# Loading the first K tiles of w_in by 64-partition DMAs, with new instruction orders, in a fused attention and MoE kernel

## The chip, the cores and the metric

The kernel runs on one core of a Trainium2 chip. The metric is the device time of one execution in microseconds (us), lower is better. A run counts as slow when it is over 1.5% above the fastest of the same kernel in its call. Engines are called as the profile calls them: PE (TensorE matmul), PEld (its weight loads), DVE (VectorE), ACT (ScalarE), POOL (GpSimd), SP (SyncE). DMA engines, sixteen of them, are separate from these; a load issued by POOL is carried by some or all of the sixteen.

## The reference, cut to what matters

```python
def _attn_ref(q, k, v, g_q, g_k):                 # 8 batches, 12 heads, 448 rows, 64 columns
    q_n, k_n = rmsnorm(q, g_q), rmsnorm(k, g_k)
    scores = q_n @ k_n.T / 8
    ...                                           # softmax over the last axis
    return attn @ v

def _moe_ref(x, w_in, w_out, alpha):              # x: (8 * 448, 768) from the attention's output
    h = x @ w_in                                  # w_in: (768, 2048)
    g = h + sin(alpha * h) ** 2 / (alpha + 1e-9)
    return g @ w_out                              # w_out: (2048, 768)
```

## The kernel before

The kernel works batch by batch. In each of eight stages PE does the scores and the attention of one batch, and between them ("fillers") the second product `g @ w_out` of the batch before. At the end of the stage stands the first product `x @ w_in` of this batch, 96 matmuls of 128 x 448. Weights are loaded once, in stage 0, beside the attention of batch 0. The f32 weights are cast to bf16 on the way, and POOL issues these loads.

```python
    def load_w_in(half, c):          # half of the 2048 columns; c: which pair of the six K tiles
        cols = slice(half * D_FF // 2, (half + 1) * D_FF // 2)
        rows = moe_w_in[c * 2 * P:(c + 1) * 2 * P, cols]
        if c:
            nc.gpsimd.dma_start(out=w_in_sb[half][:, 2 * c:2 * c + 2], in_=rows.rearrange("(p x) f -> p x f", x=2))
        else:
            for pp in range(2):
                nc.gpsimd.dma_start(out=w_in_sb[half][:, pp], in_=rows.rearrange("(hi pp d) f -> pp hi d f", hi=2, pp=2)[pp])
```

For K tiles 0 and 1 the rows of `w_in` must stand in the order in which the attention leaves its heads: partition `hi * 64 + d` of K tile `pp`. Seen from DRAM one such K tile is two blocks of 64 rows, 128 rows apart.

```python
    def first_product(b, beside):
        ORDER = (0, 1, 2, 4, 3, 5)   # K tiles 0 and 1 of four column blocks first, then 2, 4, 3, 5
        ...                          # then column blocks 4 to 15, all K tiles of each
```

The order of instructions on every engine is written out by hand, as a string of tokens for stage 0, stage 1 and the later stages. The tokens that matter here:

```python
# S: scores of one tile and their exp.  A number or f: so many filler steps (8 matmuls each).
# W00: load_w_in(0, 0); W10: load_w_in(1, 0).   q50, q51: POOL squares q, k of chunk 5.
# u50, u51: DVE sums these squares.   k30, k31: POOL multiplies by the inverse root (2 instructions "qkn" each).
STAGE_N = (
    ...
        "r3 q41 f f 1 l5 1 f S 3 u40 1 S S 5 S S u41 o7 v7 S S 5 S 2 q51 k31 f S 2 S q50 k30 2 S g4 1 u50 "
        "S 2 r4 t3 1 S z3 x7 k40 y7 z1 z2 z1 "
    ...
```

When the last filler step of a block is done, DVE evicts its PSUM banks into `osb` with a copy and an add; the banks are then free for PE's next use. DVE runs its instructions in the order of the program.

Of the kernel before, what the change touches and what calls it, by code (L numbers as in the profile page):

```python
# [17 lines left out]
try:  # L18
# [13 lines left out]
STAGE_0 = (  # L32
    (
        "L G b11 q00 u00 q01 g0 b15 r00 u01 k00 r01 D1 k01 V00 q11 u11 p00 q10 V02 W11 p011 S4 u10 q20 r1 "
        "g1 S4 q21 S1 l3 u20 S1 k11 k10 S4 u21 S g2 r2 p1 k20 S2 V01 S2 S o3 q30 W00 S W12 k21 l4 o4 D2 "
        "q40 W01 p2 l5 S1 g4 S u30 q31 W02 g3 u40 v1 q41 S v6 u31 S W10 S S3 S1 S3 x2 S S x1 S1 u41 x2 y2 "
        "q51 y3 x2 z1 z1 y2 z1 z1 q50 r4 r3 z2 z1 O00 k31 "
    ),
    "2122130230213212301301321032130132012120312031230",
# [1 line left out]
)  # L41
STAGE_1 = (
    (
        "q30 6 r2 1 S 4 S S 3 S 2 u30 S k21 1 q41 1 S 1 f S 1 k20 1 S 1 S 1 f 1 S 1 f f f S q31 p2 1 u31 "
        "f l5 S 2 g3 S 2 S r3 2 u41 k30 V10 S 1 q40 1 V11 q50 S o7 v7 1 S k31 1 u40 S 3 S 2 S S 1 x6 r4 "
        "k41 z2 q51 x1 t3 y7 z5 "
    ),
    "13230103120101013131312310202302301230123",
    {-1: 'g4 V12', 1: 'k40', 3: 'u50 g5', 5: 'l6 u51', 8: 't4 l7'},
)  # L50
STAGE_N = (
    (
        "1 r2 q31 q30 f 2 S V10 f 3 V11 f f 2 S k20 3 S 2 k21 S u31 q40 1 t2 2 S 1 f u30 g3 S 2 f S f S "
        "r3 q41 f f 1 l5 1 f S 3 u40 1 S S 5 S S u41 o7 v7 S S 5 S 2 q51 k31 f S 2 S q50 k30 2 S g4 1 u50 "
        "S 2 r4 t3 1 S z3 x7 k40 y7 z1 z2 z1 "
    ),
    "01232302102020301301320321310130210231023",
    {-1: 'l6 u51 V12', 1: 'k41', 2: 't4 l7', 3: 'g5'},
# [10 lines left out]
def kernel(  # L69
# [23 lines left out]
    nc = tc.nc  # L93
    B, H, S, D = q.shape
# [104 lines left out]
    w_in_sb = [wpool.tile([P, KT, D_FF // 2], BF16, name=f"w_in_{half}") for half in range(2)]  # L199
# [21 lines left out]
    def load_w_in(half, c):  # L221


        cols = slice(half * D_FF // 2, (half + 1) * D_FF // 2)
        rows = moe_w_in[c * 2 * P:(c + 1) * 2 * P, cols]
        if c:
            nc.gpsimd.dma_start(out=w_in_sb[half][:, 2 * c:2 * c + 2], in_=rows.rearrange("(p x) f -> p x f", x=2))
        else:
            for pp in range(2):
                nc.gpsimd.dma_start(out=w_in_sb[half][:, pp], in_=rows.rearrange("(hi pp d) f -> pp hi d f", hi=2, pp=2)[pp])  # L230

    def load_w_out(half, part):
        src = moe_w_out.rearrange("(mt p) d -> p mt d", p=P)
# [275 lines left out]
    def step(b, token):  # L509
# [6 lines left out]
        elif what == "L":  # L516
            spread_alpha()
        elif what == "W":
            load_w_in(*n)
        elif what == "O":  # L520
            load_w_out(*n)
# [85 lines left out]
```

## Time and profile before

| what | value |
|---|---|
| time, median | 430.05 us (428.12 to 430.5) |
| span of the profiled execution | 429.9 us |
| PE busy | 408.5 us, 95% |
| DVE, ACT, POOL busy | 53%, 74%, 67% |
| share of PE in the chain of waits | 84% |
| mean granted PE clock | 0.988 |

A PE that is busy 95% is the bound; the other engines matter where PE stands still. The prediction shows those places. Two more lines of before are needed, from the view of the DMA issues. Columns: what is written from what, the issuing queue, the operation and count, the KB of one load as written, and the median us from issue to landing.

```profile
w_in<-in_moe_w_in_dram POOLq DMA_DIRECT2D x4, 512.0 KB, 17.5
w_in<-in_moe_w_in_dram POOLq DMA_DIRECT2D x4, 256.0 KB, 16.5
```

The 256 KB loads are K tiles 0 and 1. They take nearly as long as loads of twice the size.

### The profile page before, as it was taken

The page shows a single profiled execution, that of the slowest core. Times are in us where ns is not written, and L with a number is a line of the kernel's source. Part 1 is how long each engine was busy: PE and PEld are TensorE (multiplying, and loading weights), DVE is VectorE, ACT ScalarE, POOL GpSimd, SP SyncE. Part 2 cuts the span into 40 slices and gives each one's busy share as a digit, 9 for nine tenths or more (in the row PEclk, how much of TensorE's full clock was granted, in tenths as well). Part 3 has the DMA queues.
Part 4 walks back from the last instruction along what each step waited for, and adds up shares of the span by engine and source line. Part 5 has one row for each costly group of instructions (what it writes and reads, how often), then busy time and mean ns, then how long its engine had stood idle before and what let it go on. Part 6 is the DMA issues. An engine that isn't in the chain of part 4 may idle for free.

```text
span 429.9 us, 14999 instructions
## 1 busy us (share of the span) xinstructions
PE 408.5 (95%) x6657; PEld 239.5 (56%) x6657; DVE 227.5 (53%) x335; ACT 316.8 (74%) x465; POOL 285.9 (67%) x269
## 2 busy tenths in 40 slices
PE   4998699999999999989999899999999999999996
PEld 2443257765576556655576356665576456665563
DVE  3775257644764466545563456645665455335511
ACT  3698188896889688976889388896889588886600
POOL 4999199799796688596794677786795785003300
PEclk9999699999999999999999899999999999999999
DMA  8899999576365643835375742837465510420022
GB/s 257 179 226 163 203 162 226 131 121 155 113 134 148 173 133 62 188 88 146 105 126 143 136 127 64 180 111 159 130 95 156 122 44 3 119 58 2 1 74 73
DMA packets 68485, 54.08 MB, mean 126 GB/s; under 512 B 39860, under 2 KB 64196, under 8 KB 68420
## 3 DMA queue, kind: packets, MB, share of 16 engines
q1 hardware_dynamic: 51378, 39.60, 35.4%
q0 software_dynamic: 16096, 11.82, 19.0%
q10 hardware_dynamic: 946, 1.70, 1.1%
q8 instruction: 52, 0.85, 0.8%
q14 instruction: 13, 0.11, 0.1%
HBM read 45.62 MB, written 11.01 MB: 132 GB/s over the span
## 4 chain that ended last, share of the span: by engine, by line
PE 84%; DMA 6%; POOL 3%; DVE 2%; ACT 2%; issue 1%; POOLq 0%; SPq 0%
PE hps L400 34%; PE ops L479 27%; PE av L360 10%; PE sc L334 6%; PE ops L460 5%; DMA w_in<-in_moe_w_in_dram 4%; POOL sq L264 2%; PE ps L242 2%; ACT expT L337 2%; DMA qk<-in_q_dram 1%; DMA small<-in_moe_alpha_dram 1%; POOL qkn L289 1%; PE tp L312 1%; DVE ms L270 1%; DVE osb L486 1%
## 5 line engine op out<-in xcount | busy, mean ns | idle before, releaser
L337 ACT ACTIVATE expT<-sc 128x896 bf16<-128x896 f32 x168 | 144.6, 918 | 15.6 <-PE sc L334 14.9
L400 PE MATMUL hps<-xT,w_in 128*128 128x448 bf16 x768 | 149.8, 357 | 6.0 <-DMA w_in<-in_moe_w_in_dram 6.0
L479 PE MATMUL ops<-w_out_sb,g_sb 64*64 64x384 bf16 x3072 | 146.1, 323 | 0.0
L386 DVE SCALAR_TENSOR_TENSOR g_sb<-s,inv_alpha_sb,hps 128x448 bf16<-128x448 f32 x128 | 81.2, 677 | 74.3 <-POOL s L381 73.8
L400 PEld LDWEIGHTS <-w_in 128*128 128x128 bf16 x768 | 75.0, 99 | 80.7 <-DMA w_in<-in_moe_w_in_dram 8.0
L378 ACT ACTIVATE s<-hps,alpha_sb 128x448 f32<-128x448 f32 x128 | 74.5, 626 | 54.1 <-PE hps L400 50.3
L381 POOL TENSOR_TENSOR s<-s 128x448 f32<-128x448 f32 x64 | 59.4, 932 | 82.3 <-ACT s L378 59.3
L479 PEld LDWEIGHTS <-g_sb 64*64 64x64 bf16 x3072 | 89.8, 107 | 39.3 <-issue 2.2
L264 POOL TENSOR_TENSOR sq<-qk 128x896 f32<-128x896 f32 x44 | 73.6, 1678 | 28.3 <-DMA qk<-in_k_dram 27.6
L289 POOL TENSOR_TENSOR qkn<-qk,inv 128x448 bf16<-128x448 f32 x80 | 73.0, 937 | 4.0 <-ACT inv L280 2.0
L334 PE MATMUL sc<-qkT 64*64 64x448 bf16 x672 | 56.9, 351 | 0.4 <-DVE qkT L319 0.2
L270 DVE TENSOR_REDUCE ms<-sq 128x14 f32<-128x896 f32 x44 | 47.0, 1079 | 16.8 <-POOL sq L264 16.8
L485 DVE COPY osb<-ops 128x384 f32<-128x384 f32 x48 | 26.7, 556 | 48.8 <-PE ops L479 48.8
L267 POOL TENSOR_TENSOR qk<-qk,gg 128x896 f32<-128x896 f32 x24 | 50.2, 2090 | 2.3 <-ACT g_sb L261 2.2
L360 PE MATMUL av<-expT,vb 64*32 64x448 bf16 (+1 forms) x1120 | 38.1, 362 | 4.3 <-DVE osb L486 4.3
L372 DVE TENSOR_TENSOR xT<-av,rec 128x896 bf16<-128x896 f32 x24 | 25.5, 1088 | 30.2 <-ACT rec L366 24.0
L383 ACT ACTIVATE s<-s 128x448 f32<-128x448 f32 x64 | 36.9, 577 | 3.0
L360 PEld LDWEIGHTS <-vb 64*32 64x32 bf16 (+1 forms) x1120 | 19.2, 97 | 19.1 <-DVE osb L486 6.4
L334 PEld LDWEIGHTS <-qkT 64*64 64x64 bf16 x672 | 20.2, 106 | 13.3 <-issue 4.5
L486 DVE TENSOR_TENSOR osb<-osb,ops 128x384 f32<-128x384 f32 x48 | 26.6, 554 | 1.7
L360 PE MATMUL av<-expT,ones 64*32 64x448 bf16 (+1 forms) x672 | 25.3, 350 | 0.2 <-ACT expT L337 0.2
L460 PE MATMUL ops<-w_out_sb,g_sb 128*128 128x384 bf16 x128 | 21.0, 326 | 0.0
(48 smaller groups left out, 186.4 us busy)
## 6 DMA issues: line engine op xcount, KB each, us to landing
out_dram<-osb SPq DMA_DIRECT2D x39, 192.0 KB, 3.4
qk<-in_q_dram SPq DMA_DIRECT2D x16, 448.0 KB, 4.5
qk<-in_k_dram SPq DMA_DIRECT2D x14, 448.0 KB, 5.2
qk<-in_q_dram SPq DMA_DIRECT2D x16, 224.0 KB, 4.6
qk<-in_k_dram SPq DMA_DIRECT2D x16, 224.0 KB, 4.9
vb<-in_v_dram POOLq DMA_DIRECT2D x16, 224.0 KB, 4.8
w_out_sb<-in_moe_w_out_dram POOLq DMA_DIRECT2D x4, 768.0 KB, 13.0
out_dram<-osb SPq DMA_DIRECT2D x26, 96.0 KB, 3.1
```

The source lines that it names most:

```text
L264: nc.gpsimd.tensor_mul(st.sq[w], qk[ci][:, w], qk[ci][:, w])
L267: eng.tensor_mul(qk[ci][:, 0], qk[ci][:, 0], gg.to_broadcast([P, 2 * NJ, D]))
L270: nc.vector.reduce_sum(st.ms[:, w, :], st.sq[w], axis=AX.X)
L289: eng.tensor_mul(n[:, :, hi, :], x[:, hi], inv[:, hi].unsqueeze(2).to_broadcast([P, NJ, D]))
L334: nc.tensor.matmul(sc[pp * 64:pp * 64 + 64, hi, :S], qkt[r, 1, j * REST:(j + 1) * REST], qkt[r, 0, :], start=True, stop=True)
L337: nc.scalar.activation(expT[c, j], sc[:, :, :S], ACT.Exp, scale=SCALE)
L360: nc.tensor.matmul(av[o, k, :S], w, expT[b * NC + c, j][r, hi, :], start=(j == 0), stop=(j == NJ - 1))
L378: nc.scalar.activation(s1, hps, ACT.Sin, scale=alpha_sb[:, m, :])
L381: nc.gpsimd.tensor_mul(s2, s1, s1)
L386: nc.vector.scalar_tensor_tensor(g_sb[:, m, (b % 2) * S:(b % 2 + 1) * S], s2, inv_alpha_sb[:, m, :], hps, op0=ALU.mult, op1=ALU.add)
L400: nc.tensor.matmul(ps[:, m % 2, :S], w_in_sb[m * 2 // MT][:, kt, m % (MT // 2) * P:(m % (MT // 2) + 1) * P], x[:, kt, :], start=(kt == ORD ...
L479: nc.tensor.matmul(st["ps"][os, r, :HALF], g_sb[rs, m, c0 + o * 64:c0 + o * 64 + 64], w_out_sb[rs, m, half * HALF:(half + 1) * HALF], star ...
```

## The change

The intent is to load K tiles 0 and 1 in a form that more DMA engines carry, and to fit the hand-made orders to it.

```diff
-            for pp in range(2):
-                nc.gpsimd.dma_start(out=w_in_sb[half][:, pp], in_=rows.rearrange("(hi pp d) f -> pp hi d f", hi=2, pp=2)[pp])
+            for hi in range(2):
+                nc.gpsimd.dma_start(out=w_in_sb[half][hi * 64:hi * 64 + 64, 0:2],
+                                    in_=rows.rearrange("(hi pp d) f -> hi d pp f", hi=2, pp=2)[hi])
```

The orders of stage N (those of stages 0 and 1 change likewise, by moved W00, W10 and score tokens):

```diff
-        "1 r2 q31 q30 f 2 S V10 f 3 V11 f f 2 S k20 3 S 2 k21 S u31 q40 1 t2 2 S 1 f u30 g3 S 2 f S f S "
-        "r3 q41 f f 1 l5 1 f S 3 u40 1 S S 5 S S u41 o7 v7 S S 5 S 2 q51 k31 f S 2 S q50 k30 2 S g4 1 u50 "
-        "S 2 r4 t3 1 S z3 x7 k40 y7 z1 z2 z1 "
+        "1 r2 q31 q30 f 2 S V10 f 3 V11 f f k20 2 S 3 S 2 k21 S u31 q40 1 t2 1 g3 1 S 1 f u30 S 2 f S f S "
+        "r3 q41 f f 1 l5 1 f S 4 u40 S S 5 S S u41 o7 v7 S S 5 S 2 q51 f S 2 S q50 k31 k30 2 S g4 1 u50 S "
+        "2 r4 t3 1 S z3 x7 k40 y7 z1 z2 z1 "
```

## The prediction

> **What bounds the kernel now.** I read the page's busy shares first: PE 95%, and the chain of waits that ended last is 84% PE, so an engine other than PE matters only where it makes PE stand still. Then the list of waits, for PE alone. Columns: who waited for whom, us in total, times, longest.
>
> ```profile
> PE hps L400 <- DMA w_in<-in_moe_w_in_dram: 6.0, 4, 4.7
> PE aps L216 <- DMA small<-in_moe_alpha_dram: 5.8, 1, 5.8
> PE av L360 <- DVE osb L486: 4.3, 4, 2.1
> ```
>
> The middle line is the start of the kernel, which the change leaves alone. The first is one place: the first product of batch 0. The third is four places: the end of the attention of batches 3 to 6. Both are where the change works.
>
> First place, PE alone in order of time (start, length, what, idle before it):
>
> ```profile
> 37.10 2.06 PE L360 MATMUL av<-expT,vb 64*32 64x448 bf16 x72
> 39.37 0.36 PE L400 MATMUL hps<-xT,w_in 128*128 128x448 bf16 x1 [0.21 <-DMA w_in<-in_moe_w_in_dram]
> 40.08 1.50 PE L400 MATMUL hps<-xT,w_in 128*128 128x448 bf16 x7 [0.35 <-DMA w_in<-in_moe_w_in_dram]
> 46.23 1.68 PE L400 MATMUL hps<-xT,w_in 128*128 128x448 bf16 x4 [4.65 <-DMA w_in<-in_moe_w_in_dram]
> 48.72 17.77 PE L400 MATMUL hps<-xT,w_in 128*128 128x448 bf16 x84 [0.82 <-DMA w_in<-in_moe_w_in_dram]
> 66.43 1.51 PE L312 MATMUL tp<-ident,qkn 64*128 64x64 bf16 x56
> ```
>
> Eight matmuls run, then 4 after a wait for K tiles 2 and 3, then 84 after a wait for K tiles 4 and 5. From 39.37 to 66.43 these 96 matmuls take 27.06 us. The same 96 take 18.27 us in the chain of every later batch but one (18.45). So the wait costs 8.8 us, more than the 6.0 that is listed as idle. The rest is the clock, which the stretches of time show (us, busy us of PE, PEld, DVE, ACT, POOL with counts, granted clock, DMA share, GB/s):
>
> ```profile
> 42.50:45.00 2.50, 0.00 (x0) 0.00 (x0) 2.50 (x5) 0.00 (x0) 1.16 (x2) 1.00 0.62 70
> 45.00:47.50 2.50, 1.27 (x4) 0.44 (x4) 0.65 (x1) 0.00 (x0) 0.00 (x0) 0.58 1.02 167
> 47.50:50.00 2.50, 1.68 (x6) 0.59 (x5) 0.00 (x0) 0.00 (x0) 0.00 (x0) 0.50 1.18 259
> 50.00:52.50 2.50, 2.50 (x9) 1.01 (x7) 0.00 (x0) 0.00 (x0) 0.00 (x0) 0.56 1.19 271
> ```
>
> While PE waits for weights, the DMA engines are not full: 70 GB/s, against 222 to 253 in each stretch from 22.5 to 37.5. So it is not bandwidth that is short; some engines of the sixteen are behind. The trace holds the sixteen completion increments of each load. Of the first 256 KB load of K tiles 0 and 1 (issued at 22.64), fourteen come between 26.8 and 27.8 us and two at 39.2 and 39.3. Of its twin (23.51) twelve come by 28.1 and four at 39.6 to 40.0. Each load queued behind them has the same four stragglers: K tiles 2 and 3 have twelve by 37.1 and four at 45.7 to 46.2; K tiles 4 and 5 twelve by 39.6 and four at 48.2 to 48.7. Four engines carry the whole megabyte of K tiles 0 and 1, and every later load waits for them.
>
> Second place, batch 4, POOL, then DVE, then PE in order of time:
>
> ```profile
> 231.96 1.68 POOL L264 TENSOR_TENSOR sq<-qk 128x896 f32<-128x896 f32 x1 [6.28 <-DMA qk<-in_k_dram]
> 233.60 1.83 POOL L289 TENSOR_TENSOR qkn<-qk,inv 128x448 bf16<-128x448 f32 x2
> 235.38 1.68 POOL L264 TENSOR_TENSOR sq<-qk 128x896 f32<-128x896 f32 x1
> ```
>
> ```profile
> 237.10 1.09 DVE L270 TENSOR_REDUCE ms<-sq 128x14 f32<-128x896 f32 x1 [3.71 <-POOL sq L264]
> 238.10 0.55 DVE L485 COPY osb<-ops 128x384 f32<-128x384 f32 x1
> 238.68 0.56 DVE L486 TENSOR_TENSOR osb<-osb,ops 128x384 f32<-128x384 f32 x1
> ```
>
> ```profile
> 239.29 3.73 PE L360 MATMUL av<-expT,vb 64*32 64x448 bf16 x88 [2.06 <-DVE osb L486]
> ```
>
> DVE waits in a reduction for POOL's second square, and the PSUM eviction behind it in DVE's queue holds the bank that PE needs. POOL was late because k landed late, and because two qkn multiplies stand ahead of that square.
>
> **What the Trainium skill says.** "DMA: Bandwidth & Descriptors", section "Why a DMA increments its semaphore by 16 and not by 1": the number of DMA engines of a load is the largest up to 16 that divides the slowest dimension (not of size 1) of both patterns, and from POOL the engines are consecutive ones from a cursor that goes round. The old source pattern has the 2 of `hi` outermost, so two engines, and the twin the next two. The trace agrees: two stragglers, then four. The page also names an exception with all 16 for some copies of POOL; this trace shows it does not apply here. "TensorE: Matmul & The Clock Gate", section "HAM oscillation — how this bites in real kernels", gives idle gaps of some 3.4 us as what halves the clock. The trace has 0.50 from 45.4 to 52.2 after an idle 4.65; but also 0.50 from 240.0 to 243.4 after an idle of only 2.06, so here the page is not quite borne out.
>
> **The change, part by part.** The order of instructions in the two kernels differs as follows: none on DVE, ACT and SP; on POOL only the shape of four loads, and in stage N the second square before the two qkn instead of behind them; on PE nothing before stage 1, then score blocks that move by one filler of 8 matmuls. The moved W00 and W10 tokens change no engine's order.
>
> (a) The loads. Same bytes and the same four POOL issues (0.85 us each), but now 64 outermost on both sides, so 16 engines. The trace has a proof of that shape: the 64-partition v loads issued at 10.96 and 11.55 have their increments at 14.2 to 14.6 and 14.9 to 16.0, no straggler. What arrives when: on the twelve light engines the queue behind gets 1/16 of a further megabyte (f32 at the source), 65 KB each. These engines took 65 KB of K tiles 4 and 5 in about 2.5 us (37.1 to 39.6), and K tiles 2, 3 with one batch of q and k (123 KB) in 5.8 us, 21 to 26 KB/us. So 2.5 to 3.1 us are added to the light engines' times: K tiles 0, 1 at about 30 (needed at 39.2), K tiles 2, 3 at 37.1 + 2.8 = 39.9 (needed at 39.2 + 8 x 0.19 = 40.7), K tiles 4, 5 at 39.6 + 2.8 = 42.4, or 41.5 if the engines keep their best rate (needed at 41.5). PE waits 0 to 1, say 0.6 us, and no longer at half clock. The second half's first K tiles come at about 45 instead of 53.6 and are needed 9 us into the product, at 48.5 or later; w_out at about 50 and 55 instead of 58.3 and 62.2, needed from 58.5. Gain 8.8 - 0.6 = 8.2 us, all on the path, since every later stage starts after it.
>
> (b) Square before the two qkn, stage N. The square moves ahead by 1.8 us (the 1.83 of the qkn pair), and so do the reduction and the eviction. The four waits of 1.14, 2.06, 0.34 and 0.76 become 0, 0.3, 0, 0: gain 4.0. In batch 4 the clock dip goes too: its 88 matmuls took 3.73 us where those of batch 3 took 2.28, and the product after it 18.45 for 18.27; gain 1.6. The qkn themselves end no later, as POOL's sum of work is unchanged and they wait for ACT anyway.
>
> (c) Score blocks one filler later. ACT is busy 39 us of a stage of 47 to 51, so a shift of 8 matmuls (0.33 us) is absorbed: 0.
>
> Sum: 8.2 + 4.0 + 1.6 = 13.8. From the median 430.05 that leaves 416.3; I take 416.5.
>
> **The rivals.** First: the DMA engines are the bound anyway, so K tiles 4 and 5 land at 44 or later and the clock dips again. For it: the DMA share is over 1.0 in the six stretches from 22.5 to 37.5, which means little room. Against it: 70 to 98 GB/s from 40 to 45, capacity that is now usable earlier. It would leave 3 to 4 us of the 8.8: about 420. Second: the wait passes on to POOL and DVE. A first product that starts early meets POOL's two squares (waiting for k, landed at 38.36) and DVE's two reductions, which now sit at 42.5 and 44.57 just as the first snake results are due at 43.7. In the trace the banks come back some 2 us before PE wants them, and DVE would be some 0.7 us later against PE, so I expect nothing; 1 to 2 us at worst, 418. Third: the 64-partition form doesn't spread, or spreads on 8 engines: no gain in (a) beyond a few us, some 421 to 424. The v loads speak against it. Fourth: the late k load in stage N is later by chance in other runs, so that the 1.8 us is not enough: 1 to 2 us lost.
>
> **Range and chances.** The central case is 416.5; a clean stage 0 and no waits in stage N give 414.5 or so, the first two rivals 418 to 420. Range 413.5 to 420.5. Faster by over 2% means under 421.5, which fails only if the loads don't spread or new waits eat 5 us: 0.9. Slower is hard to see at all: 0.01.
>
> **What would show it.** In the changed profile the landing of the w_in loads of 256 KB should drop from 16.5 us to 6 to 8, that of the 512 KB ones from 17.5 to about 11; the wait of hps for w_in from 6.0 to under 1.5; no half clock between 45 and 52; 96 matmuls of the first product in 18.3 to 19.5 us; the wait of av for osb from 4.3 to under 0.5, with two or three squares in a row ahead of the qkn; and PE busy at 97 to 98%. A wait of hps on w_in of 4 us or more, or a new PE wait on DVE g_sb or on q/k transposes, would make it wrong.

## The result, and the profile after

The changed kernel takes 417.41 us (median of 4 runs, 416.57 to 417.64), the kernel before in the same rounds 430.27 (428.12 to 436.06). The highest of its four runs is 1.9% above the lowest and so counts as slow; without it the median is 430.05. The ratio, of fast runs alone, is 0.9714, 95% interval 0.9675 to 0.9753: faster by over 2%. A ratio here is the mean time of one kernel's fast runs over that of the other's of the same rounds, so not quite the ratio of the medians. The medians of fast runs differ by 12.6 us, the two profiled spans by 15.1 (429.9 and 414.8): the profile of before is of a run of 431.65 us, slower than those timed beside it, and that of after of its fastest, 416.57.

The list of waits of the changed kernel, for PE alone (all of it):

```profile
PE aps L216 <- DMA small<-in_moe_alpha_dram: 6.0, 1, 6.0
PE sc L331 <- ACT expT L338: 0.4, 1, 0.4
PE sc L335 <- DVE qkT L320: 0.2, 1, 0.2
PE av L361 <- ACT expT L338: 0.2, 1, 0.2
```

The wait for w_in (6.0 before) and that for the eviction (4.3) are gone, and nothing stands in their place. (Lines of the file are one further down than before.) PE in order of time at the first product of batch 0:

```profile
37.44 2.06 PE L361 MATMUL av<-expT,vb 64*32 64x448 bf16 x72
39.43 18.34 PE L401 MATMUL hps<-xT,w_in 128*128 128x448 bf16 x96
57.70 1.51 PE L313 MATMUL tp<-ident,qkn 64*128 64x64 bf16 x56
```

One unbroken run of 96 matmuls; the four runs with waits between them before ended at 66.43. The stretches of time from 42.5 on (columns as in the prediction):

```profile
42.50:45.00 2.50, 2.50 (x15) 1.31 (x14) 2.50 (x5) 1.16 (x3) 2.34 (x4) 1.00 0.39 27
45.00:47.50 2.50, 2.50 (x15) 1.30 (x14) 2.50 (x4) 2.45 (x5) 1.78 (x3) 1.00 1.17 178
47.50:50.00 2.50, 2.50 (x15) 1.27 (x13) 1.03 (x3) 2.01 (x5) 2.48 (x4) 1.00 1.25 237
```

PE does 15 matmuls in each stretch at a clock of 1.00, where it did 0, 4 and 6 with the clock falling to 0.50. The DMA engines move only 27 GB/s from 42.5 to 45; the last increment of w_in comes at 43.4. PE is busy 97% of the span, as predicted. The view of the DMA issues:

```profile
w_in<-in_moe_w_in_dram POOLq DMA_DIRECT2D x4, 512.0 KB, 9.0
w_in<-in_moe_w_in_dram POOLq DMA_DIRECT2D x4, 256.0 KB, 6.0
```

Both sizes got faster, the 512 KB loads too, whose code is the same (for 256 KB 6 to 8 us were predicted, for 512 KB about 11). Batch 4's end of attention, POOL, DVE and PE in order of time:

```profile
221.60 3.32 POOL L265 TENSOR_TENSOR sq<-qk 128x896 f32<-128x896 f32 x2 [5.75 <-DMA qk<-in_k_dram]
224.87 3.63 POOL L290 TENSOR_TENSOR qkn<-qk,inv 128x448 bf16<-128x448 f32 x4
```

```profile
224.95 1.09 DVE L271 TENSOR_REDUCE ms<-sq 128x14 f32<-128x896 f32 x1 [1.39 <-POOL sq L265]
225.95 0.55 DVE L486 COPY osb<-ops 128x384 f32<-128x384 f32 x1
226.53 0.56 DVE L487 TENSOR_TENSOR osb<-osb,ops 128x384 f32<-128x384 f32 x1
```

```profile
227.22 2.27 PE L361 MATMUL av<-expT,vb 64*32 64x448 bf16 x88
```

POOL still waits nearly 6 us for k, but does both squares at once. DVE's reduction waits 1.39 instead of 3.71 us, the eviction ends at 227.09, and PE goes on at 227.22 without a gap.

Where the 15.1 us of the two spans come from, by the starts of the first and last matmul of each first product in the traces: the last matmul of batch 0 starts at 57.41 instead of 66.14, 8.7 us. The seven stretches from one first product to the next took 29.64, 29.53, 30.66, 33.03, 29.86, 30.28 and 29.33 us and take 29.80, 29.60, 29.33, 29.33, 29.42, 29.33 and 29.33, together 6.2 less. The product of batch 4 is 0.2 shorter. The stretch behind the last product is the same, 25.35.

### The profile page after: what moved, and what is told of

It is laid out like the page before. It is cut to its first block, busy times and chain, and to the rows that moved or that the text cites. A ratio compares the mean times of both kernels' runs of the same rounds, so it can differ in the third digit from the quotient of the medians.

```text
span 414.8 us, 14996 instructions
## 1 busy us (share of the span) xinstructions
PE 403.4 (97%) x6657; PEld 238.9 (58%) x6657; DVE 227.2 (55%) x335; ACT 316.8 (76%) x465; POOL 285.0 (69%) x269
## 3 DMA queue, kind: packets, MB, share of 16 engines
q0 software_dynamic: 12512, 11.81, 19.3%
## 4 chain that ended last, share of the span: by engine, by line
PE 94%; ACT 3%; DMA 1%; issue 0%; DVE 0%; POOLq 0%
PE hps L401 35%; PE ops L480 30%; PE av L361 13%; PE sc L335 7%; PE ops L461 5%; ACT expT L338 3%; PE ps L243 2%; DMA small<-in_moe_alpha_dram 1%; PE sc L331 1%; PE tp L313 1%; ACT rec L367 0%; ACT rec L366 0%; PE aps L216 0%; DVE osb L466 0%; PE gps L209 0%
## 5 line engine op out<-in xcount | busy, mean ns | idle before, releaser
L338 ACT ACTIVATE expT<-sc 128x896 bf16<-128x896 f32 x168 | 144.6, 918 | 15.7 <-PE sc L335 15.1
L401 PE MATMUL hps<-xT,w_in 128*128 128x448 bf16 x768 | 146.7, 353 | 0.0
L265 POOL TENSOR_TENSOR sq<-qk 128x896 f32<-128x896 f32 x44 | 73.4, 1677 | 29.0 <-DMA qk<-in_k_dram 27.9
L361 PE MATMUL av<-expT,vb 64*32 64x448 bf16 (+1 forms) x1120 | 36.8, 350 | 0.1
```

What stands on the lines that cost most here:

```text
L265: nc.gpsimd.tensor_mul(st.sq[w], qk[ci][:, w], qk[ci][:, w])
L338: nc.scalar.activation(expT[c, j], sc[:, :, :S], ACT.Exp, scale=SCALE)
L361: nc.tensor.matmul(av[o, k, :S], w, expT[b * NC + c, j][r, hi, :], start=(j == 0), stop=(j == NJ - 1))
L401: nc.tensor.matmul(ps[:, m % 2, :S], w_in_sb[m * 2 // MT][:, kt, m % (MT // 2) * P:(m % (MT // 2) + 1) * P], x[:, kt, :], start=(kt == ORD ...
```

## The experiments

Twelve kernels ran with 5 rounds each, so 6 runs of each. Ratios are to the kernel before. Its median was 430.10, 431.64, 430.92 and 429.35 us in the four calls, so medians of different calls are compared with care. A profile is that of one run, and in e2, e4 and e9_outer4 it was the slowest of the six.

**e1_loads: the new loads alone.** The changed kernel with the three stage orders of before.

```diff
 # against the changed kernel: STAGE_0, STAGE_1, STAGE_N as in the kernel before
```

> The new loads with the old orders of all stages. My theory: the whole gain of stage 0 (the end of the first product of batch 0 moves from 66.1 to 57.4 us) comes from the loads, and the waits of PE for the eviction at the end of batches 3 to 6 stay (0.3 to 2.1 us each, some 4 in all). So about 421.5 us, ratio to before 0.980, PE idle for w_in 0. Rival (the gain of stage 0 needs the moved W00 and W10 tokens too): no or little gain, 428 or more.

Measured: 421.23 us (419.42 to 422.28), ratio 0.9788 (0.9744 to 0.9831). In its profile PE runs the first product of batch 0 unbroken (last matmul at 57.20), and this wait is left:

```profile
PE av L361 <- DVE osb L487: 2.6, 3, 1.3
```

As expected; the moved W00 and W10 tokens aren't needed for the gain of stage 0.

**e2_orders: the new orders alone.**

```diff
-            for hi in range(2):  ...64-partition form...
+            for pp in range(2):  ...the form of before...
```

> The old loads with the new orders. My theory: the wait for w_in stays as before (about 6 us idle, first product of batch 0 26.8 us long, clock at 0.5 for 6.8 us), the waits for the eviction are gone. So about 426 us, ratio 0.990. With e1 the two gains add up to that of the change (12.9 us). Rival (the two parts hang together, say, the late waits come from the DMA backlog of stage 0): the late waits stay and the time is that of before.

Measured: 426.56 us (426.01 to 429.44), ratio 0.9921 (0.9880 to 0.9963). Its list of waits has the w_in wait of before, and no line of PE waiting for the eviction:

```profile
PE hps L400 <- DMA w_in<-in_moe_w_in_dram: 6.9, 4, 3.2
```

(In this run half clock lasts 13.7 us; 6.8 was expected.) The gains of the two parts add up: 0.9788 times 0.9921 is 0.9711, and the whole change has 0.9714. In medians the loads are worth 8.9 us and the orders 3.5.

**e3_contig128: is it the 64 partitions, or the outermost dimension?** The old form, 128 partitions and one K tile per load, but with 128 consecutive source rows each. Its output is wrong, which doesn't matter for the time.

```diff
-            for hi in range(2):  ...64-partition form...
+            for pp in range(2):
+                nc.gpsimd.dma_start(out=w_in_sb[half][:, pp], in_=rows.rearrange("(pp p) f -> pp p f", pp=2)[pp])
```

> Wrong result on purpose. The changed kernel, but K tiles 0 and 1 loaded by the old form, two DMAs of 128 partitions x 1024, only with 128 consecutive source rows each, so that the outermost source dimension is 128 and not 2. My theory (the outermost dimension of the source sets how many DMA engines carry the load): as fast as the changed kernel, 417.4 within 1, the sixteen increments of these loads within 2 us of each other, no wait for w_in. Rival (64 partitions, or both K tiles in one DMA, are what helps): stragglers and the wait as before, 425 or so.

Measured: 417.29 us (417.03 to 417.72), ratio 0.9697 (0.9661 to 0.9733). The increments of the first of these loads come between 26.8 and 29.0 us, of the second between 28.7 and 31.2 (2.2 and 2.5 us apart, a little over the 2 expected); PE never waits for w_in. The 64 partitions as such do nothing. What counts is the outermost dimension of the source, 2 before, 128 here.

**e9_outer4: four engines per load?** As e3, with four blocks of 32 rows.

```diff
+            for pp in range(2):
+                nc.gpsimd.dma_start(out=w_in_sb[half][:, pp], in_=rows.rearrange("(g pp d) f -> pp g d f", g=4, pp=2)[pp])
```

> Wrong result on purpose. The old form with the 128 source rows as 4 blocks of 32, outermost dimension 4. My theory: 4 engines per load, 8 for the pair, each with 128 KB of source; eight stragglers in the loads queued behind, some 2.8 us late, so K tiles 4 and 5 land at about 43.3 us (40.5 in the changed kernel, 48.7 before), PE waits 1.5 to 2 us for them, at full or part clock: 419 to 420.5 us. Rival (any outermost dimension under 16 falls back to two engines or to one form): as with the old loads, 426; rival (128 partitions in one DMA spread anyway): 417.4.

Measured: 422.15 us (420.02 to 425.16), ratio 0.9815 (0.9769 to 0.9861). Four engines per load, as expected: the first load has twelve increments by 27.9 us and four at 35.0 to 36.3; the load of K tiles 4 and 5 has eight by 43.8 and eight at 46.9 to 47.4. But that is 47.4, not 43.3, and PE waits 4.4 us, and the clock is at half for 6.8 us from 46.0 on. The count of engines was right and the time missed. The trace's packets show slow rows: one row (4 KB read, 2 KB written) takes an engine 172 to 173 ns in the median of each kernel shown so far, and here the median in slices of 2 us from 28 to 36 us is 212 to 305 ns.

**e10_outer4_odd: why were the rows slow?** The same four blocks of 32 rows, 33 rows apart instead of 64.

```diff
+                nc.gpsimd.dma_start(out=w_in_sb[half][:, pp], in_=rows[124 * pp:124 * pp + 132].rearrange("(g e) f -> g e f", g=4)[:, :32])
```

> Wrong result on purpose. The old form with 4 blocks of 32 source rows as in the run with outermost dimension 4, but the blocks 33 rows (264 KB) apart instead of 64 rows (512 KB). In that run the rows took 242 to 305 ns (median of 2 us slices) where all other kernels show 173, and that is why it was slower than I expected. Theory: source blocks a power of two apart slow one another; here rows take 173 ns, 32 of them 5.5 us, K tiles 4 and 5 land at about 43.3, and the time is 419 to 420.5. Rival (four engines per load are slow in themselves): 422 as there, rows of 240 ns and more.

Measured: 421.12 us (418.97 to 423.95), ratio 0.9762 (0.9714 to 0.9809). The median row is back at 172 to 173 ns in every slice, though in one slice the slowest tenth of the rows takes 324 or more. K tiles 4 and 5 land at 45.2 and PE waits 2.8 us for w_in. So the slow median row goes with the distance of the blocks, in one profile each. It is not any power of two that does it: in the kernel before the blocks are 1 MB apart, two engines a load, and the median row is 172 to 173 ns in every slice from 26 to 42 us. The two ratios' intervals overlap, so the times don't settle it, and why 45.2 is still 1.9 us over what I expected stays open. Part of the spread is the clock: the two runs at 423.8 and 424.0 have a mean clock of 0.992, the four others 0.996 to 0.999.

**e9_outer8: eight engines per load.** As e9_outer4 with `g=8`.

> Wrong result on purpose. Outermost dimension 8, blocks 32 rows (256 KB) apart. By the rule of the outermost dimension each load takes 8 engines, the pair all 16, 16 rows each as in the changed kernel: 417.4 within 1 if only the number of rows per engine counts. If blocks a power of two apart slow one another: rows of over 200 ns in these loads, K tiles 4 and 5 at 42 to 44, 418 to 420.

Measured: 419.81 us (417.86 to 420.11), ratio 0.9712 (0.9679 to 0.9744). The pair of loads is spread over all sixteen engines (last increments 28.9 and 30.8), K tiles 4 and 5 land at 41.9 and PE waits 1.0 us. The median row is 172 to 173 ns, but the slowest tenth takes at least 245 to 313 ns in the slices from 30 to 36 us, where this limit is 172 to 173 in the changed kernel. So the profile lies between the two expectations, and the times don't decide: 419.81 us fits the second, the ratio is that of the changed kernel (0.9714). From two to four and eight engines per load the time falls with the rows on the fullest engine (64, 32 and 16 of a pair of loads): 426.56, 422.15 and 419.81 us with the new orders.

**e4_w10_old: does the second half of the columns matter?** The changed kernel with the old form for `half == 1` only.

```diff
+        elif half == 1:
+            for pp in range(2):  ...the form of before...
```

> The changed kernel with the old load form for the second half of w_in alone (K tiles 0 and 1 of columns 1024 and up). An engine takes 173 ns for a row in the traces, so 64 rows on each of four engines take 11.1 us from some 40.7 on: landing at about 52, needed at 39.4 + 9 = 48.4. My theory: PE now waits there for 3 to 4 us in the middle of the first product, and w_out, queued behind, may add 1 to 2 us at the start of stage 1, so 421 to 423. Rival (the second half has time to spare, since before it was never waited for): 417.4.

Measured: 424.31 us (423.47 to 427.12), ratio 0.9818 (0.9775 to 0.9861). Worse than expected by 1 to 3 us. PE at the first product of batch 0:

```profile
41.72 7.07 PE L404 MATMUL hps<-xT,w_in 128*128 128x448 bf16 x36 [0.85 <-DMA w_in<-in_moe_w_in_dram]
54.36 0.55 PE L404 MATMUL hps<-xT,w_in 128*128 128x448 bf16 x1 [5.57 <-DMA w_in<-in_moe_w_in_dram]
56.83 11.08 PE L404 MATMUL hps<-xT,w_in 128*128 128x448 bf16 x47 [1.92 <-DMA w_in<-in_moe_w_in_dram]
```

The old form lands at 54.3 and 56.8 us here, 52 expected. The packets of this trace account for the later one: from 42 to 57 us a row took 188 ns in the mean (173 is the median), and the engines also started 32 packets of q and k each, of 90 ns, which the expectation left out. 64 x 0.188 + 32 x 0.090 is 14.9 us, from 41.7, when K tiles 4 and 5 of the first half had landed, to 56.6. Before, these loads landed at 51.4 and 53.6, and no one waited, because PE was stalled for the first half until 48.7. One stall hid the next. Both halves have to be changed.

**e5_swap: of the orders, only the second square ahead of the qkn.** New loads, old orders, one move:

```diff
-... S S 5 S 2 q51 k31 f S 2 S q50 k30 2 S g4 1 u50 ...
+... S S 5 S 2 q51 f S 2 S q50 k31 k30 2 S g4 1 u50 ...
```

> The new loads, the old orders, and of the new orders only the second square ahead of the two qkn in stage N. My theory: this one swap is the whole gain of the orders, so as the changed kernel, 417.4 within 1 us, PE's waits for the eviction under 1 us in sum. Rival (the moved score blocks give it): 421.2 as with the new loads alone.

Measured: 417.31 us (416.64 to 418.78), ratio 0.9659 (0.9621 to 0.9697), and no wait of PE for the eviction in the profile. This one swap is the whole gain of the new orders, as far as the spread lets one see.

**e7_scores: the new orders without that swap.**

```diff
-... S S 5 S 2 q51 f S 2 S q50 k31 k30 2 S g4 1 u50 S "
+... S S 5 S 2 q51 k31 f S 2 S q50 k30 2 S g4 1 u50 S "
```

> The changed kernel with the swap of stage N taken back, so new loads and the moved score blocks alone. My theory: the score moves are worth nothing, so as the new loads alone, 421.2 within 1, with the waits for the eviction (2 to 4 us in sum). Rival: 417.4.

Measured: 423.22 us (419.72 to 425.60), ratio 0.9783 (0.9733 to 0.9833), as with the loads alone (0.9788), with waits for the eviction of 5.4 us in sum:

```profile
PE av L361 <- DVE osb L487: 5.4, 3, 2.2
```

The median is 2 us above what I expected, within the spread of this kernel; the ratio is that of e1. The moved score blocks are worth nothing that shows.

**e6_u50_late: a failed experiment.** The reduction `u50` moved two tokens back, past `S 2`, with new loads and old orders.

```diff
-... q50 k30 2 S g4 1 u50 S 2 r4 t3 1 S z3 ...
+... q50 k30 2 S g4 1 S 2 u50 r4 t3 1 S z3 ...
```

> The new loads, the old orders, POOL's order as before, but the one reduction of stage N that waits for POOL's second square stands behind the two evictions of the next filler in DVE's queue. My theory (PE waits because the eviction stands behind that reduction in DVE's queue): the waits of PE for the eviction go, 417.4 within 1, though POOL's squares are as late as before. Rival (POOL being late delays PE in another way, or the reduction's own result is needed soon): 420 or more.

Measured: 421.44 us (419.82 to 425.30), ratio 0.9768 (0.9719 to 0.9817), with 5.9 us of waits for the eviction. It says nothing on the theory: no eviction falls between the two places, so every engine's order is that of e1. As a repeat of e1 it shows that the late waits differ from run to run (2.6 and 5.9 us in two profiles of the same order).

**e11_u50_last: the same test done properly.** `u50` behind the last filler step, so behind the last eviction in DVE's queue; POOL as before.

```diff
-... q50 k30 2 S g4 1 u50 S 2 r4 t3 1 S z3 ...
+... q50 k30 2 S g4 1 S 2 r4 t3 1 u50 S z3 ...
```

> What the run with the reduction moved by two tokens failed to do (no eviction fell between the two places, so its instruction order was that of the new loads alone). Here, new loads, old orders, POOL's order as before, and in stage N the one reduction that waits for POOL's second square stands behind the last eviction in DVE's queue. My theory (PE waits only because the eviction stands behind that reduction): PE's waits for the eviction are 0 though POOL's squares are as late as before, and the time is 417.4 within 1. Rival (late POOL delays PE in another way): 420 to 423, with another wait in place of the one for the eviction.

Measured: 416.57 us (416.13 to 417.42), ratio 0.9694 (0.9661 to 0.9728). No wait of PE for the eviction. POOL's second square is as late as before, yet DVE evicts first, batch 4, POOL and DVE in order of time:

```profile
222.38 1.83 POOL L290 TENSOR_TENSOR qkn<-qk,inv 128x448 bf16<-128x448 f32 x2
224.17 1.68 POOL L265 TENSOR_TENSOR sq<-qk 128x896 f32<-128x896 f32 x1
```

```profile
225.59 0.56 DVE L486 COPY osb<-ops 128x384 f32<-128x384 f32 x1 [1.70 <-PE ops L480]
226.18 0.55 DVE L487 TENSOR_TENSOR osb<-osb,ops 128x384 f32<-128x384 f32 x1
226.65 1.08 DVE L271 TENSOR_REDUCE ms<-sq 128x14 f32<-128x896 f32 x1
```

The square still stands between the two qkn pairs, and the copy starts 0.26 us before it ends (225.85). So PE waited only because the eviction stood behind a reduction that it does not depend on.

**e12_both: the changed kernel with this move as well.**

```diff
-... q50 k31 k30 2 S g4 1 u50 S 2 r4 t3 1 S z3 ...
+... q50 k31 k30 2 S g4 1 S 2 r4 t3 1 u50 S z3 ...
```

> The changed kernel with that reduction behind the last eviction as well: a try for a better one. The changed kernel has no PE wait left in its profile, but up to 0.7 us came back in other runs with its orders when k landed late. My theory: 416.5 to 417.3, at most 0.5 us better than the changed kernel (417.4), and a narrower spread. Rival: the reduction now delays the xT multiplies behind it, 418 or more.

Measured: 416.85 us (416.24 to 416.93), ratio 0.9698 (0.9669 to 0.9728). It and e11 have the lowest medians of all, 0.6 and 0.8 us under the changed kernel. But the changed kernel did not run in that call, whose kernel before was also 0.7 us faster than the fast runs of that of the result (429.35 and 430.05). The narrow spread is as expected; that e12 beats the changed kernel is not shown.

## Why the prediction was right

416.5 was predicted and 417.41 measured, inside 413.5 to 420.5 and on the side given a chance of 0.9. Of the gain of 13.8 us 12.6 came. The mechanism was right in both places; that the sum is so near is in part luck, since (a) was reckoned too small and (b) too large.

**What bounds it, and the four engines.** Right, and shown by e3 and the two counts between: the outermost dimension of the source sets the number of engines. The traces confirm it a second way. POOL's DMA queue has 16,096 packets before, 12,512 after and in e3, 14,048 in e9_outer4 and 13,024 in e9_outer8:

```profile
q0 software_dynamic: 12512, 11.81, 19.3%
```

The line is that of the changed kernel's page (packets, MB, share of the engines' time). The excess is packets of 4 bytes, and its size fits 2, 4 and 8 engines: 3,584 is 4 loads x 14 unused engines x 64, 1,536 is 4 x 12 x 32, and 512 is 4 x 8 x 16. In e4, where two loads have the old form, it is 1,792, which is 2 x 14 x 64.

**(a) the loads, 8.2 us.** Right in mechanism, a little small: 8.9 in e1, and 8.7 in the pair of profiles. The term that was mis-sized is the 0.6 us that PE should still wait for K tiles 4 and 5. In the changed kernel's profile they land at 40.5 us and not at 41.5 to 42.4, K tiles 2 and 3 at 37.3 and not at 39.9. The prediction added the new rows to the light engines' times as if these had been full. They were not: from 30 to 34 us the engines started 140 rows of w_in before and 281 after. A better working, after the fact: 64 rows per engine (16 of each of four pairs of K tiles) at 173 ns and 32 packets of q and k at 87 ns make 13.9 us from about 27, so 40.9. For before, with 64 + 48 rows on the fullest engines, it gives 49.2 where 48.7 was measured. The margin is thin all the same: in e4, where this half is loaded by the new form too, K tiles 4 and 5 land at 41.7 and PE waits 0.85 us for them.

**(b) the swap, 5.6 us.** The four waits went as worked out (e5, e7, e11). The size was too large in three comparisons of four: 3.5 us in e2's call, 3.8 between the medians of e1 and of the changed kernel in different calls, 4.1 between e6 and e5 in one call (e6 has e1's order, so these two differ by the swap alone), and 5.9 between e7 and e5. Two things make it vary. How late k lands differs from run to run (2.6 and 5.9 us of waits in e1 and e6). And the clock dip of 1.6 us in batch 4 was counted as if every run had it. The mean clocks of e1 and e6 show that not every run does: ten of their twelve runs have 0.998 or more and two, both of e6, 0.994. One of these two is the profiled one, with 3.4 us of half clock in batch 4 after a wait of 3.12. The new orders narrow the spread too: 416.57 to 417.64 against 419.42 to 425.30 in e1 and e6.

**(c) score blocks, 0.** Right (e5 and e7).

**The rivals.** The DMA-bound one fell: the first product has no wait at all. The passing on to DVE fell too: the second of DVE's reductions starts at 44.91 (44.57 was reckoned) and the first result of the snake right behind it, at 45.90, and PE does not wait for the bank. The form that does not spread fell with the 6.0 us landing. Late k came back as 0.7 us in one profile with the new orders (e3, batch 4), the kind of loss the fourth rival names.

**The statement that the second half is needed at 48.5 or later** held, but the prediction did not say what follows from it: with the first half repaired, the second half's old form stalls PE for 7.5 us (5.57 and 1.92 in the profile of e4, whose run was 2.8 us above its median).

## What to carry to other kernels

When a load is slow and the DMA engines as a whole are not full, look at its completion increments one by one: a few stragglers were the sign here that a short outermost dimension (2) kept the load on few engines, and that all loads queued behind it waited for these. Put a large dimension outermost on both sides; 64 and 128 gave all sixteen here. In a queue that runs in order, place an eviction that frees PSUM ahead of a reduction that waits for another engine. Repair all loads of one kind together, since one stall can hide the next.

## What the Trainium skill lacked or had wrong

- "DMA: Bandwidth & Descriptors", section "Why a DMA increments its semaphore by 16 and not by 1": its rule for the number of engines held for outermost dimensions 2, 4, 8, 64 and 128 on loads from POOL with a cast. It leaves open when its exception (all 16 for some copies of POOL) applies; loads of 128 partitions with an outer dimension of 2, 4 and 8 did not get it. Beside the data the page has a completion descriptor per engine and a least number of packets for a small transfer, but not what the runs show: 3,584 more packets of 4 bytes in the kernel before, a number that fits as many on each unused engine as a used one has rows (64).
- The same page, section "Latency and other measured facts": of copies with rows a large power of two apart it gives 207 GB/s at 512 KiB and only 103 at 4 MiB. Here blocks of rows 512 KB apart, each read by its own engine, had median rows of 212 to 305 ns against 173 (e9_outer4), and 172 to 173 at 264 KB (e10_outer4_odd), so a smaller distance seems able to hurt more than the page lets one expect. The two are not the same case (the page's copies were issued by the sync and scalar queues), blocks 1 MB apart in the kernel before had 172 to 173, and the cause is not shown.
- "TensorE: Matmul & The Clock Gate", section "HAM oscillation — how this bites in real kernels": idle gaps of about 3.4 us are its limit. Here gaps of 2.06 us (before, batch 4) and 3.12 (e6) were followed by half clock and one of 2.19 was not (e7), so the length of one gap alone does not tell.
- No page gives the time of one row of a load with a cast on one DMA engine, which was the useful number here (the first page has a bandwidth per engine): 172 to 173 ns in the median for 4 KB of f32 read and cast to 2 KB.
